# Seven block products in place of eight in the network stages of the last 2048 tokens, on one Trainium2 core

## The chip, the cores and the metric

The kernel runs on one core of one Trainium2 chip. The metric is device time in microseconds (us) for one execution; lower is better. The kernel before was timed in three runs.

## The reference, cut to what matters

The inputs are q, k and v of shape (4 batches, 8 heads, 768 tokens, 64) and four network weights. Attention comes first, then a network over all 4 x 768 = 3072 tokens:

```
k_sum = k.reshape(B, H, nb, 32, D).max(axis=3);  v_sum = v.reshape(B, H, nb, 32, D).mean(axis=3)
scores_l = scale * q @ k^T          masked to |i - j| < 16
scores_s = scale * q @ k_sum^T + log(32)
a = softmax(concat(scores_l, scores_s))
x = a @ concat(v, v_sum)            -> (3072 tokens, 512)
h = (x @ w1) * (x @ w2)             -> (3072, 1024)
out = (h @ w3) @ w_out              -> (3072, 512)
```

Everything is float32. The kernel folds `w3 @ w_out` into one matrix once, so that the network has two stages: the gates (`x @ w1`, `x @ w2` and their product) and the projection (h times the folded matrix). Each float32 operand of a network matmul is kept as two float32r numbers, a rounded one (hi) and the rest (lo), and each product is the sum of three matmuls: hi x hi, lo x hi and hi x lo.

## The kernel before, in words

The 3072 tokens are cut into six units of 512 tokens, and attention into 24 steps: a step is one unit and one pair of heads (`place` at L528 divides the step number by 4).

**Attention step.** `begin` (L549) makes the score matmuls on PE. `reduce` (L340) adds the mask and takes the extreme of each row on DVE, `expose` (L356) takes the exponential on ACT, `invert` (L363) adds 1e-9 on POOL and takes the reciprocal on DVE, and `normalize` (L367) multiplies on POOL. Two steps later come `transposes` (L381) on PE, `evacuate` (L391) to SBUF on ACT and DVE, `outputs` (L400) on PE, and `keep_x` (L417), which writes x as hi (ACT) and lo (DVE, `low` at L108). The inputs of a step arrive on SP's DMA queue: `fetch` (q and k), `fetch_values` (v). `load_sums` (L294) copies the block means of v into the value tile on POOL, and `gather` (L316) the block maxima of k into the key tile, on POOL as well.

**Network.** `gate` (L427) takes 128 of the 1024 gate columns of one unit: 12 matmuls with w1 (4 chunks of 128 inputs, three each), an ACT copy out of PSUM (L448), 12 matmuls with w2, the product on DVE (L453), then hi on ACT (L454) and lo on DVE. Eight such calls make a unit's gates. `project` (L459) makes 128 tokens of output in 24 matmuls over the eight chunks of the folded matrix `wp`, an ACT copy (L472) and a store issued on ACT's queue (L473); four calls make a unit. All of these matmuls have 512 columns and go through `products` (L111), so their line in the profile is L113. A unit has 192 gate matmuls and 96 projection matmuls. All network weights stay in SBUF as hi and lo.

**Order.** PE's order is written out. `run(columns)` (L520) draws network matmuls from a generator until so many columns have been handed out. In the first loop (L716), a schedule by turns (`LOADS`, `WORK`) loads and converts the weights, folds `w3 @ w_out` and makes the first eight attention steps, with unit 0's network filling in. In the second loop (L760), two attention steps are made together: both transposes, both scores, both outputs, then about 144 network matmuls. The order on the other engines is by priority, except for the attention instructions of ACT and DVE, which keep their program order. SP's order is written out in the first loop only; POOL's in the second only.

## Time and profile before

| | |
|---|---|
| runs of the kernel before | 534.08, 532.41, 533.48 us; median 533.48 us |
| profiled execution, first to last instruction (span) | 533.5 us |
| TensorE clock granted, mean | 0.990 |
| PE busy | 511.2 us (96%) |
| DVE, ACT, POOL busy | 240.6, 225.4, 95.9 us |
| moved by DMA | 68.78 MB, mean 129 GB/s |

Only the span is given for the profiled execution itself; it equals the median of the runs to 0.02 us. In the profile, PE is TensorE's matmuls, PEld its weight loads, DVE is VectorE, ACT ScalarE, POOL GpSimd, and SP the engine that issues most DMAs. Busy times of overlapping matmuls are merged, so that the mean of one matmul (391 ns) is longer than the distance between two of them; the distance is read from the chain of waits.

### The profile page before, as it was taken

The numbers are of one execution on the slowest core, as the hardware profiler recorded it, in microseconds if no ns is written. First come the engines' busy times: TensorE is split into PE (matmuls) and PEld (weight loads), VectorE is DVE, ScalarE is ACT, GpSimd is POOL, SyncE is SP. The second block draws the span as 40 slices with busy tenths as digits, with TensorE's granted clock in tenths as the row PEclk, the third lists the DMA queues.
The fourth block names the chain that finished last, engine by engine and source line by source line (L and its number), as shares of the span: only waits on it lengthen the run. The fifth ranks groups of instructions, "written<-read, shape, count | busy, mean of one in ns | idle before, by whom it ended". The sixth has DMA issues, their size and how long they took to land.

```text
span 533.5 us, 9766 instructions
## 1 busy us (share of the span) xinstructions
PE 511.2 (96%) x3888; PEld 421.4 (79%) x3888; DVE 240.6 (45%) x667; ACT 225.4 (42%) x627; POOL 95.9 (18%) x158
## 2 busy tenths in 40 slices
PE   1889989999999999999999999999999999999997
PEld 0667767888888888888888888888888888888885
DVE  5889987798534326435244043251042350222210
ACT  5587964674626226135154063361172361222210
POOL 2020635001033202305005014014023031000000
PEclk9989997999999999999999999999999999999999
DMA  8995699804834013453040150050150011100001
GB/s 346 413 411 220 252 325 413 316 2 139 274 131 167 0 55 122 151 172 134 0 177 1 60 195 1 1 177 20 49 187 2 14 69 40 39 3 0 1 20 59
DMA packets 21166, 68.78 MB, mean 129 GB/s; under 512 B 2304, under 2 KB 2432, under 8 KB 18560
## 3 DMA queue, kind: packets, MB, share of 16 engines
q1 hardware_dynamic: 17664, 61.86, 31.6%
q10 hardware_dynamic: 3456, 6.29, 3.1%
q8 instruction: 30, 0.49, 0.4%
q14 instruction: 16, 0.13, 0.1%
HBM read 61.85 MB, written 6.29 MB: 128 GB/s over the span
## 4 chain that ended last, share of the span: by engine, by line
PE 87%; DMA 5%; DVE 4%; ACT 2%; issue 1%; POOL 0%; SPq 0%; POOLq 0%; ACTq 0%
PE mm L113 76%; PE po L408 4%; PE sc L331 4%; DMA rows<-in_vP_dram 2%; PE tp L388 2%; DVE wf L176 2%; DMA wraw<-in_w_dram 1%; DVE w L109 1%; DMA wraw<-in_wo_dram 1%; ACT sm L359 1%; DVE wf L173 1%; ACT wf L164 1%; DVE sm L345 0%; ACT w L190 0%; DVE ks L236 0%
## 5 line engine op out<-in xcount | busy, mean ns | idle before, releaser
L113 PE MATMUL mm<-x,w 128*128 128x512 f32 x1152 | 264.3, 391 | 0.0
L113 PEld LDWEIGHTS mm<-x,w 128*128 128x128 f32 x1152 | 216.5, 188 | 45.3
L113 PE MATMUL mm<-wp,h 128*128 128x512 f32 x576 | 133.3, 390 | 0.0
L113 PEld LDWEIGHTS mm<-wp,h 128*128 128x128 f32 x576 | 107.7, 188 | 22.6
L359 ACT ACTIVATE sm<-sm,mx 128x120 f32<-128x120 f32 x192 | 73.6, 385 | 16.3 <-DVE mx L345 16.3
L453 DVE TENSOR_TENSOR g<-mm,g 128x512 f32<-128x512 f32 x48 | 33.1, 690 | 88.7 <-PE mm L113 85.4
L454 ACT CAST h<-g 128x512 fp32r<-128x512 f32 x48 | 29.5, 618 | 90.6 <-DVE g L453 90.6
L113 PE MATMUL mm<-w,w 128*128 128x512 f32 x192 | 51.2, 419 | 14.8 <-ACT w L190 12.0
L113 PEld LDWEIGHTS mm<-w,w 128*128 128x128 f32 x192 | 37.3, 200 | 25.7 <-ACT w L190 12.7
L364 POOL TENSOR_SCALAR mx<-mx 128x8 f32<-128x8 f32 x24 | 6.8, 283 | 275.5 <-ACT sm L359 275.3
L472 ACT COPY o<-mm 128x512 f32<-128x512 f32 x24 | 14.0, 584 | 82.5 <-PE mm L113 82.5
L397 DVE COPY pt<-tp 120x512 f32<-120x512 f32 x22 | 14.3, 684 | 75.2 <-PE tp L388 75.2
L109 DVE TENSOR_TENSOR h<-g,h 128x512 fp32r<-128x512 f32 x48 | 35.2, 736 | 25.6 <-ACT h L454 25.4
L448 ACT COPY g<-mm 128x512 f32<-128x512 f32 x48 | 28.1, 586 | 39.0 <-PE mm L113 38.4
L298 POOL COPY v<-vs 24x512 f32<-24x512 f32 (+1 forms) x64 | 40.7, 635 | 8.9 <-DMA v<-in_vW_dram 5.9
L345 DVE CUSTOM_DVE_ANT_0 sm<-sc,mask_sb 128x120 f32<-128x120 f32 x192 | 41.1, 274 | 0.0
L359 ACT ACTIVATION_READ_ACCUMULATOR sm<-sm,mx 128x1 f32 x192 | 36.2, 188 | 0.0
L368 POOL TENSOR_TENSOR sm<-sm,mx 128x960 f32<-128x960 f32 x16 | 28.7, 1793 | 5.6 <-DVE mx L365 5.6
L109 DVE TENSOR_TENSOR x<-po,x 128x512 fp32r<-128x512 f32 x24 | 16.6, 690 | 28.6 <-ACT x L419 28.5
L190 ACT CAST w<-wf 128x1024 fp32r<-128x1024 f32 (+1 forms) x22 | 21.3, 968 | 17.3 <-DVE wf L176 17.2
L408 PEld LDWEIGHTS po<-pt,v 120*64 120x64 f32 x768 | 24.5, 141 | 4.0 <-issue 2.5
L408 PE MATMUL po<-pt,v 120*64 120x64 f32 x768 | 26.6, 228 | 0.9 <-POOL v L298 0.5
(35 smaller groups left out, 287.9 us busy)
## 6 DMA issues: line engine op xcount, KB each, us to landing
v<-in_vW_dram SPq DMA_DIRECT2D x24, 512.0 KB, 6.4
wraw<-in_w3T_dram SPq DMA_DIRECT2D x8, 1024.0 KB, 13.0
wraw<-in_w_dram SPq DMA_DIRECT2D x8, 1024.0 KB, 9.3
k<-in_kW_dram SPq DMA_DIRECT2D x20, 368.0 KB, 5.3
raw<-in_kT_dram SPq DMA_DIRECT2D x16, 392.0 KB, 3.7
q<-in_qG_dram SPq DMA_DIRECT2D x24, 256.0 KB, 4.9
raw<-in_vB_dram SPq DMA_DIRECT2D x12, 512.0 KB, 3.8
out_dram<-o ACTq DMA_DIRECT2D x24, 256.0 KB, 2.0
```

The costliest lines, as they stand in the source:

```text
L109: eng.tensor_tensor(dst, src, hi.bitcast(F32), ALU.subtract)
L113: nc.tensor.matmul(acc, lhsT=a, rhs=b, start=first and i == 0, stop=last and i == len(terms) - 1)
L190: nc.scalar.copy(t[:, 0, some], f[:, some])
L298: nc.gpsimd.tensor_copy(v[at : at + NB, g, blocks], src.unsqueeze(1).broadcast_to([NB, n, P]))
L331: nc.tensor.matmul(sc[h][64 * g : 64 * g + 64, i * KR : (i + 1) * KR], lhsT=q[rows, i * P + 64 * g : i * P + 64 * g + 64], rhs=k[rows, i, ...
L345: nc.vector.tensor_tensor_reduce(out=sm[:, j], in0=sc[h][:, i * KR : (i + 1) * KR], in1=mask_sb[:, 0 if blk == 0 else 2 if blk == BLOCKS - ...
L359: nc.scalar.activation(sm[:, j], sm[:, j], AF.Exp, bias=mx[:, 0, j : j + 1], scale=-1.0, accum_out=mx[:, 1, j : j + 1])
L368: nc.gpsimd.tensor_tensor(sm, sm, mx[:, 2].unsqueeze(2).broadcast_to([P, NI, KR]), ALU.mult)
L408: nc.tensor.matmul(po[cols, at : at + 64], lhsT=v[:KR, g, i, cols], rhs=pt[g][:, (h * NBLK + i) * 64 : (h * NBLK + i + 1) * 64], start=Tru ...
L448: nc.scalar.copy(g, a[:, :U])
L453: nc.vector.tensor_tensor(g, acc[1][:, :U], g, ALU.mult)
L454: nc.scalar.copy(h[:, 0], g)
```

## The change

Units 0 and 1 (the first 1024 tokens) keep the network of before. Units 2 and 3 are taken together, and so are units 4 and 5. For such a couple, both network stages become a product of two by two blocks: the gates have w1 and w2 as the two rows of blocks, the two halves of the 512 inputs as the inner index and the two units as the columns; the projection has the two halves of the output columns, the two halves of the 1024 gate columns, and the two units. A product of two by two blocks takes eight block products; here it takes seven, at the price of sums of blocks before and after:

- **Weight sums** (`stationary`, `sums_of_gates`, `sums_of_output`): four sums per tile of blocks on POOL, split into hi (ACT) and lo (DVE), stored to DRAM. The plain blocks are stored too (`spill_weights`, `spill_wp`, `whole_wp`, and the line added to `convert`).
- **x** of units 2 to 5 goes out of PSUM through one ACT copy to DRAM (`spill_x`) and is loaded again (`load_x`). `moving_x` makes the seven moving operands: for four of the seven a POOL sum, then hi (ACT) and lo (DVE).
- **Gates** (`fast_gates`): two rounds, each with seven products in four lanes (a lane is one PSUM bank), six matmuls per lane and product. The weights come from DRAM, two tiles of 512 KB per product, asked for in advance by `flow_in`. After each product each bank is read out (`evacuated`): by ACT for the first two products, by DVE with an addition for the other five. A bank goes on accumulating within the groups (0, 1), (2, 3) and (4, 5, 6) of products. POOL multiplies the two gates.
- **Projection** (`fast_project`): seven products in two lanes of twelve matmuls; the moving operands for the next product are made during this one (`moving_h`). The output is transposed, stored by SP into a second output tensor.
- **Attention steps** of the second loop are taken one at a time (`lump`): transposes and scores, 12 network matmuls, outputs, then more network matmuls. `invert` and `gather` move from POOL to DVE. The block means of v of the later batches go to the value tile by DMA from DRAM (`keep_means`, `fetch_means`). POOL's and SP's order is no longer written out in the second loop.

The core of the diff:

```
@@ convert
         for some in parts:
             low(nc.vector, t[:, 1, some], f[:, some], t[:, 0, some])
+        if name in wR:
+            nc.sync.dma_start(wR[name][i], f)
...
+    def spill_x(po, u, c):
+        t = sb.tile([P, U], F32, name="xr", tag="wf", bufs=5)
+        nc.scalar.copy(t, po[:, :U])
+        nc.sync.dma_start(xS[u][c], t)
...
+    def moving(k, b, dst):
+        hi, lo = dst
+        src = b[(0, 1, 0, 1, 0, 0, 1)[k]][(0, 0, 0, 1, 0, 1, 0)[k]]
+        if k == 2:
+            nc.gpsimd.tensor_tensor(src, b[0][1], src, ALU.subtract)
+        elif k == 3:
+            nc.gpsimd.tensor_tensor(b[0][1], src, b[0][1], ALU.subtract)
+        elif k == 4:
+            nc.gpsimd.tensor_tensor(src, b[1][1], src, ALU.subtract)
+        elif k == 6:
+            nc.gpsimd.tensor_tensor(src, src, b[0][0], ALU.subtract)
+        yield 1
+        nc.scalar.copy(hi, src)
+        yield 1
+        low(nc.vector, lo, src, hi)
...
+    def flow_in(n):
+        while flow and len(ready) < n:
+            t = sb.tile([P, 2, 512], F32R, name="ws", tag="x", bufs=6)
+            nc.sync.dma_start(t.bitcast(F32), flow.pop(0))
+            ready.append(t)
+
+    def lanes(n, weights_of, moving_of, steps, evacuated, tags, between=None):
+        banks = [ps.tile([P, 512], F32, name="ln", tag=tag, bufs=bufs) for tag, bufs in tags]
+        for k in range(NK):
+            stationary_of = yield from weights_of(k)
+            for i in range(n):
+                for c in range(steps):
+                    if between and c % KH == 0:
+                        between(k, i * steps // KH + c // KH)
+                    a, m = [stationary_of(i, c, w) for w in range(2)], moving_of(k, c)
+                    terms = [(a[0], m[0]), (a[1], m[0]), (a[0], m[1])]
...
+                with tc.high_priority(offset=SOONER):
+                    evacuated(k, i, banks[i][:, :U])
...
+    def fast_gates(n):
...
+            def weights_of(k):
+                while (n, k) not in xT:
+                    yield -1
+                flow_in(4 if r == NF // 4 - 1 and k >= 4 else 6)
+                two = [ready.pop(0), ready.pop(0)]
...
+            def evacuated(k, i, got):
...
+                if k < 2:
+                    nc.scalar.copy(h[:, 0] if k else p1, got)
+                else:
+                    to, more = ((p5, p1), (h[:, 1], p1), (h[:, 1], h[:, 1]), (p5, p5), (p1, p1))[k - 2]
+                    nc.vector.tensor_tensor(to, got, more, ALU.add)
+                if k == 5:
+                    nc.gpsimd.tensor_tensor(h[:, 1], h[:, 1], p5, ALU.mult)
+                elif k == 6:
+                    nc.gpsimd.tensor_tensor(h[:, 0], h[:, 0], p1, ALU.mult)
...
+    def fast_project(n, hr):
...
+        def weights_of(k):
+            flow_in(4)
...
+        def evacuated(k, i, got):
...
+            done = {1: (0, 0, c11), 4: (0, 1, d), 5: (1, 1, p5), 6: (1, 0, p1)}
+            if k in done:
...
+                nc.sync.dma_start(outT[rows : rows + P, cols : cols + U], t)
...
     def network():
-        for u in range(NU):
+        for u in range(2):
...
+        for n in range(1, NSU):
+            raws = yield from fast_gates(n)
+            yield from fast_project(n, raws)
...
+    CLASSIC = ALL_FOLD + 2 * UNIT
+    FAST = 3 * U * 4 * KH
+    UP_TO = {p: TO_SLOTS + (CLASSIC - TO_SLOTS) * (p - NFIRST + 1) / NFIRST for p in range(NFIRST, 2 * NFIRST)}
+    UP_TO[2 * NFIRST] = CLASSIC + 1.2 * FAST
+    UP_TO[2 * NFIRST + 1] = CLASSIC + 2.9 * FAST
+    for p in range(2 * NFIRST + 2, NS + 2):
+        UP_TO[p] = UP_TO[p - 1] + 2.2 * FAST
...
+    def lump(p):
...
+            tp = transposes(sms.pop(p - 2)[0], **more)
+            pt = evacuate(tp)
+            b = begin(p) if p < NS else None
...
+        run(given[0] + 12 * U)
+        with tc.manual_schedule(engines={engines.Activation, engines.DVE}):
+            finish_step(p - 2, pt, **more)
...
+        run((given[0] + UP_TO[p]) / 2)
+        load_batch()
+        run(UP_TO[p])
```

FAST is the 24 matmuls of one gate product. The sums and the operands of x are made in small pieces, one each time 2048 columns have been handed to PE (`tend`); the order in which they are asked for is tied to the attention step (`EXTRA`: sums of the gates from step 8, x of units 2 and 3 from step 12, x of units 4 and 5 from step 21).

More of the change, by code (lines that the diff above doesn't have):

```diff
@@ L398, in evacuate, with outputs @@
         return pt
[L400 to L402 removed]
+    def outputs(pt, v, **more):
+        po = ps.tile([P, 512], F32, name="po", **more or {"tag": "tp", "bufs": 2})
         for i in range(NBLK):
@@ new lines, in finish_step, with work_on @@
+    def finish_step(p, pt, **more):
+        u, c = place(p)
+        po = outputs(pt, values.pop(p), **more)
+        if u < 2:
+            keep_x(po, xs[u])
+        else:
+            spill_x(po, u, c)
+    def work_on(u, sm, mx, sc):
+        for h in range(2):
+            reduce(u, h, sc, sm, mx)
+            expose(h, sm, mx)
+        invert(mx)
+        normalize(sm, mx)
+    CLASSIC = ALL_FOLD + 2 * UNIT
+    FAST = 3 * U * 4 * KH
+    UP_TO = {p: TO_SLOTS + (CLASSIC - TO_SLOTS) * (p - NFIRST + 1) / NFIRST for p in range(NFIRST, 2 * NFIRST)}
@@ L795, in attention_moe @@
+    with tc.manual_schedule(engines=MANUAL):
+        for p in range(NFIRST, NS + 2):
+            lump(p)
         run(float("inf"))
-_OUT = "out_0_dram"
+_OUT, _OUT_T = "out_0_dram", "out_1_dram"
 def kernel(q, k, v, moe_w1, moe_w2, moe_w3, moe_w_out):
```

340 lines of the change are left out of this document (263 added, 77 removed).

## The prediction, made before the changed kernel was run

> **What bounds the kernel now.** I read the page first (busy times, the forty slices, the chain that ended last), then the chain in order of time, the groups of instructions with shapes apart, the time line of DVE and POOL where they overlap, and the DMA issues.
>
> ```profile
> span 533.5 us, 9766 instructions
> ...
> PE 511.2 (96%) x3888; PEld 421.4 (79%) x3888; DVE 240.6 (45%) x667; ACT 225.4 (42%) x627; POOL 95.9 (18%) x158
> ...
> PE   1889989999999999999999999999999999999997
> ...
> GB/s 346 413 411 220 252 325 413 316 2 139 274 131 167 0 55 122 151 172 134 0 177 1 60 195 1 1 177 20 49 187 2 14 69 40 39 3 0 1 20 59
> ...
> PE 87%; DMA 5%; DVE 4%; ACT 2%; issue 1%; POOL 0%; SPq 0%; POOLq 0%; ACTq 0%
> ```
>
> PE is busy for nine tenths or more of every slice from the seventh to the last but one, and 87% of the last chain is PE. The chain in order of time shows what the second loop does:
>
> ```profile
> 382.99 1.09 PE tp L388 x32
> 384.08 1.98 PE sc L331 x64
> 386.06 2.02 PE po L408 x64
> 388.08 32.86 PE mm L113 x144
> ...
> 462.38 67.60 PE mm L113 x297
> 530.00 0.59 ACT o L472
> ```
>
> Two attention steps cost PE 1.09 + 1.98 + 2.02 = 5.1 us, so one costs 2.55. Behind them 144 network matmuls take 32.86 us without a gap: **228.2 ns each**. Here nothing but the number of PE's instructions sets the time, so a matmul removed is worth its full distance, as long as PE stays fed.
>
> ```profile
> L113 PE MATMUL mm<-x,w 128*128 128x512 f32 x1152 | 264.3, 391 | 0.0
> L113 PE MATMUL mm<-wp,h 128*128 128x512 f32 x576 | 133.3, 390 | 0.0
> L453 DVE TENSOR_TENSOR g<-mm,g 128x512 f32<-128x512 f32 x48 | 33.1, 690 | 88.7 <-PE mm L113 85.4 <-ACT sm L359 1.6 <-ACT wf L164 1.3
> L109 DVE TENSOR_TENSOR x<-po,x 128x512 fp32r<-128x512 f32 x24 | 16.6, 690 | 28.6 <-ACT x L419 28.5
> L454 ACT CAST h<-g 128x512 fp32r<-128x512 f32 x48 | 29.5, 618 | 90.6 <-DVE g L453 90.6
> L448 ACT COPY g<-mm 128x512 f32<-128x512 f32 x48 | 28.1, 586 | 39.0 <-PE mm L113 38.4
> L368 POOL TENSOR_TENSOR sm<-sm,mx 128x960 f32<-128x960 f32 x16 | 28.7, 1793 | 5.6 <-DVE mx L365 5.6
> L318 POOL COPY k<-ks 128x96 f32<-128x96 f32 x16 | 5.3, 350 | 23.6 <-DMA k<-in_kW_dram 21.0 <-DVE ks L236 2.2
> L364 POOL TENSOR_SCALAR mx<-mx 128x8 f32<-128x8 f32 x24 | 6.8, 283 | 275.5 <-ACT sm L359 275.3
> ```
>
> **What is removed.** The first two rows are 1152 + 576 = 1728 matmuls, 288 per unit. A couple of units takes 576; with seven products it takes 7/8 of that, 504 (two gate rounds of 7 x 4 lanes x 6, and 7 x 2 lanes x 12). Two couples save 2 x 72 = 144 matmuls of the same shape: 144 x 0.2282 = **32.9 us**. Attention's matmuls stay. So PE alone would give 533.5 - 32.9 = 500.6 us. The sum is made against the span of 533.5, which is also the median of the runs (533.48), so nothing is converted.
>
> A couple then lasts 504 x 0.2282 = 115.0 us on PE, one product (24 matmuls) 5.48 us, a projection (168) 38.3 us.
>
> **What is added beside PE.** Per couple I count on DVE 14 lows of x, 28 lows of h, 40 additions out of PSUM in the gates and 10 in the projection: 92, where two units of before have 40. At 0.69 us each (the two DVE rows above) that is 63.5 us in 115. On ACT: 14 + 28 casts, 16 + 4 copies and 8 for the spilled x, 70 x about 0.61 = 43 us. On POOL, 8 sums for x, 16 for h and 16 gate products: 40. The trace has no POOL operation of two full tiles of 512; the nearest is the normalization of 960 columns at 1793 ns, and by columns 512 take 0.96 us (an estimate), 38 us per couple. Each engine alone fits beside 115 us of PE. Two things do not follow from such sums: who blocks whom, and whether data arrives.
>
> **POOL against DVE.** The time line of the two engines:
>
> ```profile
> 207.03 1.79 POOL L368 TENSOR_TENSOR sm<-sm,mx 128x960 f32<-128x960 f32 x1 [0.81 <-DVE mx L365]
> 212.72 1.79 POOL L368 TENSOR_TENSOR sm<-sm,mx 128x960 f32<-128x960 f32 x1 [0.32 <-DVE mx L365]
> 280.92 1.79 POOL L368 TENSOR_TENSOR sm<-sm,mx 128x960 f32<-128x960 f32 x1 [0.32 <-DVE mx L365]
> ```
>
> ```profile
> 207.52 1.85 DVE L109 TENSOR_TENSOR h<-g,h 128x512 fp32r<-128x512 f32 x1
> 213.88 1.18 DVE L109 TENSOR_TENSOR h<-g,h 128x512 fp32r<-128x512 f32 x1 [0.69 <-ACT h L454]
> 281.97 0.69 DVE L453 TENSOR_TENSOR g<-mm,g 128x512 f32<-128x512 f32 x1
> ```
>
> A low from SBUF normally takes 0.69 us. Begun while POOL normalizes it takes 1.85 and 1.18, and ends at 209.37 and 215.06, both times 0.55 us after POOL's end (208.82, 214.51). It does not run slower; it waits for POOL. The gate product, with one input in PSUM, is untouched at 0.69 under the third normalization. The Trainium skill has this as a rule (page "SBUF — State Buffer", section "Who interferes with whom"): a DVE instruction with two SBUF inputs and a GpSimd instruction that reads SBUF exclude each other, the later one waiting to the end of the earlier. By that rule, the trace agrees, with the 0.55 us above.
>
> The change puts both kinds into the same stretch. In a projection, 28 lows (19.3 us) and 16 POOL sums (15.3 us) exclude each other: 34.6 us in 38.3 of PE. If DVE's 10 additions (6.9) never ran under a POOL sum, DVE would need 41.5 us, 3.2 too many. In the first couple's projection, four steps' normalizations (4 x 1.79) and the x operands of the next couple (2 POOL sums, 6 lows: 6.1) add 13.3 us against 4 x 2.55 = 10.2 of attention on PE: 3.1 more. Bounds: 0 to 3.2 + 6.3 = 9.5 us. I take **2**, near zero, because POOL can run a product ahead, and the additions can run under its sums.
>
> **The weight stream.** Weights now come from DRAM twice per couple: 21 products of two 512 KB tiles, 22 MB in 115 us, 191 GB/s. The page shows slices of 413, so the mean fits. What matters is the wait for a buffer. Of six buffers the gates use two per product and are two products ahead (11 us). From the last gate products on, and through the projection, `flow_in(4)` keeps one product ahead: a pair is asked for when PE has freed the pair before, and needed one product, 5.48 us, later. I count 10 such pairs in the first couple and 8 in the second.
>
> ```profile
> v<-in_vW_dram SPq DMA_DIRECT2D x24, 512.0 KB, 6.4
> wraw<-in_w_dram SPq DMA_DIRECT2D x8, 1024.0 KB, 9.3
> ...
> raw<-in_vB_dram SPq DMA_DIRECT2D x12, 512.0 KB, 3.8
> out_dram<-o ACTq DMA_DIRECT2D x24, 256.0 KB, 2.0
> ```
>
> ```profile
> 69.52 0.42 SPq L144 DMA_DIRECT2D wraw<-in_w_dram  x1
> ```
>
> Alone, 512 KB land in 3.8 us; the second tile streams behind the first, 0.52 MB at 413 GB/s = 1.27 us, so the pair takes 5.1, or 5.5 with one issue of 0.42 on SP: just on time. In the congested first loop 1024 KB took 9.3 us, 3.8 too late. Ends: 0 and 18 x 3.8 = 68 us. Near the lower end, since most of that stretch has little other traffic. But SP's queue is in order: the output stores of products 1, 4 and 5 wait for a copy of 0.59 us and take two issues, and the load behind them starts about 1.2 us late. Six such loads: **+7.2 us**.
>
> **x by way of DRAM.** The last x of a couple goes ACT copy 0.59, store 2.0, load 3.5 (256 KB; between the 2.0 of a 256 KB store and the 3.8 of a 512 KB load, nearer the load), POOL 0.96, cast 0.62, low 0.69: 8.4 us, and the fourth product needs it. PE has, after those outputs, 29 matmuls of its step (1.7 x 24 less the 12 ahead of the outputs, 6.6 us), the next step's transposes and scores (1.5) and about 2 matmuls (0.5): 8.6 us. If the cover fails altogether it costs 8.4; I take **+1**. The second couple has three products in front, 16 us: nothing.
>
> **The first loop.** `gather` and `invert` move to DVE, which stands here:
>
> ```profile
> 93.00:133.00 40.00, 40.00 (x178) 33.13 (x177) 35.13 (x75) 23.73 (x56) 3.00 (x6) 1.00 0.43 156
> ```
>
> ```profile
> 109.30 1.23 DVE L109 TENSOR_TENSOR w<-wf,w 128x1024 fp32r<-128x1024 f32 x1
> 110.44 1.22 DVE L176 SCALAR_TENSOR_TENSOR wf<-wraw,wf 128x1024 uint32<-128x1024 uint32 x1
> ```
>
> DVE is busy 35.1 of 40 us and converts gate weights back to back just ahead of their use. A few gathers and additions (0.35 and 0.28 on POOL) go in front: 0 to 3 us, I take **+1**. SP's eight new stores of the converted weights wait for DVE, with the next weight loads behind them; those have three tiles' conversion in front, so nothing. The block-mean copies that POOL loses only shorten its queue. Taking attention steps singly costs PE nothing of its own, and 12 matmuls (2.7 us) cover the copies between transposes and outputs; with that cover gone it would be at most 1 us a step. At the end the last bank leaves by a DVE addition (0.69) where ACT copied (0.59): 0.1, left out.
>
> **Sum:** 533.5 - 32.9 + 2 + 7.2 + 1 + 1 = 511.8: **512 us**.
>
> **The rivals.**
> (a) *Everything stays hidden.* Pairs land in time and the sums fall in POOL's free time: 500.6 + 1 + 1 = 502.6. For it: the 5.1 us pair, DMA nearly idle in the last slices of before; against it: SP's order. 0.18. The Trainium skill (page "SBUF — State Buffer", section "The DMA setup-cost knee") fits 2 us plus bytes over 436 GB/s, 4.4 us for a pair by my estimate; the stream's term would then be near 0. No 1 MB load here ran alone to test it.
> (b) *The exclusion binds.* A lane's bank must be read out within 12 matmuls (2.74 us). An addition on DVE behind two lows that each wait for a POOL sum takes 2 x (0.96 + 0.55) + 0.69 = 3.7, 1 us late. Half of the 28 lane read-outs of both projections late by 1 us is 14 in place of 2: 524. For it: 34.6 of 38.3 us; against: POOL may run ahead. 0.18.
> (c) *Slower: the one-ahead weight stream is late at every product.* If a 512 KB tile lands in v's 6.4 us, which it took in company with q and k, a pair takes 7.7, 2.2 late, 18 times: 39.6 in place of 7.2, so 544. It turns to a loss where a pair takes over 5.48 + (533.5 - 504.6)/18 = 7.1 us. For it: attention's 1.1 MB per step and x share the engines in the first couple. Against: from then on, little shares them. 0.10.
> (d) *The products do not pay as counted*, for a matmul distance above 228 ns between alternating tiles: the shape is the same, so 0.02, and I put it at no change.
>
> **How the numbers follow.** My forecast has 0.52, from 505 to 518. A change within 0.3% (1.6 us) is about what a measurement cannot tell from none. Faster: 0.52 + 0.18 + 0.18 = 0.88; same 0.02; slower 0.10. The range reaches down to (a) and up past (b) by part of the x cover: 502 to 530; only (c) stays out, and what would go beyond either end.
>
> **What would show it.** PE instructions 3888 - 144 = 3744, the last row of the chain at 228 ns per matmul within a product. The stream's term: PE waiting in the projections for DMA of `ws`, about 1 us at the third, sixth and seventh product, none in the gates. The exclusion's: lows of 1.2 to 1.7 us and waits of PE for DVE. I am wrong if PE waits in the gates, if matmuls inside a product stand over 230 ns apart, or if the first 135 us shift by more than 3.

## The result, and the profile after

| | before | after |
|---|---|---|
| runs beside each other, median of 4 | 533.75 us (532.41 to 534.08) | 584.85 us (583.62 to 587.61) |
| profiled execution, span | 533.5 us | 584.2 us |
| TensorE clock granted, mean | 0.990 | 0.951 |

The ratio is 1.097, with a 95% interval from 1.093 to 1.101: slower by 10%, where 512 us and a range of 502 to 530 were forecast. The page of the changed kernel:

```profile
span 584.2 us, 10335 instructions
...
PE 506.2 (87%) x3744; PEld 401.5 (69%) x3744; DVE 378.5 (65%) x851; ACT 260.4 (45%) x695; POOL 218.2 (37%) x174
...
PE   2989979999948999895398999897979899999797
...
PEclk9989989999977999999599999998999899999899
...
GB/s 353 409 414 230 198 366 411 231 214 364 366 358 167 278 229 349 241 357 398 249 312 260 236 316 305 342 303 231 252 181 248 260 202 190 192 203 101 145 179 155
```

PE has 3744 instructions, as forecast, and is now busy for 87% of the span. A slice is 14.6 us: the big holes are the twelfth (161 to 175 us) and the nineteenth and twentieth (263 to 292 us), and in the last of these the granted clock is down at half. The GB/s row, which before had slices at 1 and 2 GB/s, stands above 100 everywhere; the bytes went from 68.78 to 157.64 MB. What PE waited for, by the view of waits (total, times, longest):

```profile
PE sc L361 <- DVE k L348: 19.7, 5, 6.8
...
PE ln L627 <- ACT xT L558: 9.6, 1, 9.6
PE ln L627 <- DVE tmp L751: 7.0, 4, 2.9
...
PE ln L627 <- ACT tmp L748: 4.1, 1, 4.1
```

L361 are the score matmuls, and L348 is `gather`, the copy of the block maxima into the key tile. L627 are the matmuls of the seven products, L558 the cast of x and h to hi, L751 and L748 the read-outs of a bank in the projection. No row names the stream of weights (`ws`). Groups of instructions, shapes apart (the last but one number of the first part is the mean, in ns, as in the prediction's rows):

```profile
L125 DVE TENSOR_TENSOR hT<-hr,hT 128x512 fp32r<-128x512 f32 x56 | 59.6, 1101 | 23.9 <-ACT hT L558 23.6
...
L398 POOL TENSOR_TENSOR sm<-sm,mx 128x960 f32<-128x960 f32 x16 | 30.0, 1875 | 67.4 <-DVE k L348 24.8 <-issue 19.6 <-ACT h L489 9.5
...
L554 POOL TENSOR_TENSOR hr<-hr 128x512 f32<-128x512 f32 x8 | 13.6, 1727 | 9.3 <-DVE hT L125 9.3
...
L593 POOL TENSOR_TENSOR wr<-wr 128x512 f32<-128x512 f32 x6 | 7.7, 1280 | 0.5
```

The low of h before was this row:

```profile
L109 DVE TENSOR_TENSOR h<-g,h 128x512 fp32r<-128x512 f32 x48 | 35.2, 736 | 25.6 <-ACT h L454 25.4
```

A low of h takes 1101 ns in the mean where it took 736 before, and a sum of two full tiles on POOL 1280 to 1727 ns, where 0.96 us was estimated.

Where the time went shows when the span is cut at PE's first matmul of each stage. "Counted" is the prediction's 500.6 us: the time before up to unit 0's projection, then the network matmuls left at 228.2 ns each and 49.8 us of attention, split by the steps that a stage holds. The last three columns are experiments, told below.

| stage | counted | after | sums on DVE | and no weight sums | and gather on POOL |
|---|---|---|---|---|---|
| up to unit 0's projection | 129.7 | 134.2 | 137.7 | 133.4 | 130.0 |
| from there to couple 1's first product | 114.7 | 154.9 | 147.0 | 124.2 | 122.6 |
| couple 1 (units 2 and 3, with attention) | 137.7 | 167.1 | 161.5 | 163.6 | 157.7 |
| couple 2 (units 4 and 5, no attention) | 115.0 | 123.9 | 115.0 | 115.0 | 115.0 |
| rest | 3.5 | 4.1 | 4.1 | 4.2 | 4.3 |
| span | 500.6 | 584.2 | 565.3 | 540.4 | 529.6 |

Of the 83.6 us that are too many, 40 lie between unit 0's projection and the first product, before any of the new products has run. The two holes in order of time (start, duration, engine; in brackets the idle time before and what ended it):

```profile
120.29 3.81 SPq L211 DMA_DIRECT2D w<-wf  x2
124.15 2.61 SPq L766 DMA_DIRECT2D wS<-w  x3
126.80 2.59 SPq L772 DMA_DIRECT2D p<-wp  x2
...
153.28 2.18 SPq L803 DMA_DIRECT2D pR<-wpr  x2
...
158.72 0.72 SPq L328 DMA_DIRECT2D k<-in_kW_dram  x1
...
165.40 0.38 DVE L348 COPY k<-ks 128x96 f32<-128x96 f32 x1 [4.40 <-DMA k<-in_kW_dram]
165.84 1.88 PE L361 MATMUL sc<-k,q 64*64 64x120 f32 x32 [5.59 <-DVE k L348]
...
270.92 1.26 POOL L591 TENSOR_TENSOR wr<-wr 128x512 f32<-128x512 f32 x1 [10.98 <-DMA wr<-w]
...
272.87 3.40 DVE L125 TENSOR_TENSOR sp<-wr,sp 128x512 fp32r<-128x512 f32 x2 [4.28 <-ACT sp L582]
273.49 2.23 POOL L398 TENSOR_TENSOR sm<-sm,mx 128x960 f32<-128x960 f32 x1
...
276.79 0.74 DVE L348 COPY k<-ks 128x48 f32<-128x48 f32 x2
...
277.54 1.88 PE L361 MATMUL sc<-k,q 64*64 64x120 f32 x32 [6.78 <-DVE k L348]
...
282.87 2.43 SPq L651 DMA_DIRECT2D xraw<-xS  x2
...
289.06 4.35 PE L627 MATMUL ln<-xT,ws 128*128 128x512 f32 x12 [9.65 <-ACT xT L558]
```

First hole: from 120.29 to 155.46 SP issues 34 stores of weights and nothing else. They take it 35.2 us with its own waits, and the key tile of step 8 is asked for behind them at 158.72. DVE idles until it lands, and PE with it. In the kernel before, the time line of SP has it at 140.01:

```profile
140.01 0.43 SPq L308 DMA_DIRECT2D k<-in_kW_dram  x1
```

The stores start so late because eight of them, those of the converted gate weights (L211, two of them among the 34), wait for DVE's conversion, and SP's queue with them:

```profile
SPq L211 <- DVE wf L192: 27.3, 5, 7.4
```

Second hole: the last gate weights come back from DRAM late, POOL's sums of them begin at 270.92, and two lows of those sums take 3.40 us on DVE, since they and POOL's normalization exclude each other (they end at 276.27, 0.55 us after its end at 275.72, the distance that the prediction found in the kernel before). The key copy of the next step stands behind them on DVE. Then x: its first loads are issued at 282.87, because `load_x` waits in one list behind the weight sums, and the first product begins at 289.06.

### The profile page after: what moved, and what is told of

It is laid out like the page before. It is cut to its first block, busy times and chain, and to the rows that moved or that the text cites. A ratio compares the mean times of both kernels' runs of the same rounds, so it can differ in the third digit from the quotient of the medians.

```text
span 584.2 us, 10335 instructions
## 1 busy us (share of the span) xinstructions
PE 506.2 (87%) x3744; PEld 401.5 (69%) x3744; DVE 378.5 (65%) x851; ACT 260.4 (45%) x695; POOL 218.2 (37%) x174
## 2 busy tenths in 40 slices
DMA packets 56964, 157.64 MB, mean 270 GB/s; under 512 B 5968, under 2 KB 14672, under 8 KB 54352
## 5 line engine op out<-in xcount | busy, mean ns | idle before, releaser
L627 PE MATMUL ln<-xT,ws 128*128 128x512 f32 x672 | 161.9, 400 | 18.2 <-ACT xT L558 9.6
L627 PEld LDWEIGHTS ln<-xT,ws 128*128 128x128 f32 x672 | 127.2, 192 | 48.4 <-ACT xT L558 10.6
L129 PE MATMUL mm<-x,w 128*128 128x512 f32 x384 | 93.0, 400 | 0.9 <-DVE w L125 0.9
L627 PE MATMUL ln<-hT,ws 128*128 128x512 f32 x336 | 82.1, 402 | 9.3 <-ACT tmp L748 4.1
L129 PEld LDWEIGHTS mm<-x,w 128*128 128x128 f32 x384 | 72.7, 192 | 18.2 <-DVE w L125 1.6
L627 PEld LDWEIGHTS ln<-hT,ws 128*128 128x128 f32 x336 | 64.0, 193 | 25.2 <-DVE tmp L751 5.4
L125 DVE TENSOR_TENSOR hT<-hr,hT 128x512 fp32r<-128x512 f32 x56 | 59.6, 1101 | 23.9 <-ACT hT L558 23.6
L558 ACT CAST hT<-hr 128x512 fp32r<-128x512 f32 x56 | 33.0, 622 | 58.7 <-POOL hr L713 42.7
L709 DVE TENSOR_TENSOR tmp<-ln,tmp 128x512 f32<-128x512 f32 x48 | 32.9, 687 | 38.3 <-PE ln L627 24.8
L129 PE MATMUL mm<-wp,h 128*128 128x512 f32 x192 | 46.9, 399 | 1.5 <-ACT g L483 1.3
L361 PE MATMUL sc<-k,q 64*64 64x120 f32 x768 | 28.3, 289 | 20.7 <-DVE k L348 19.7
L129 PEld LDWEIGHTS mm<-wp,h 128*128 128x128 f32 x192 | 35.9, 190 | 10.7 <-ACT g L483 1.8
L361 PEld LDWEIGHTS sc<-k,q 64*64 64x64 f32 x768 | 22.3, 145 | 23.6 <-DVE k L348 13.6
```

What stands on the lines that cost most here:

```text
L125: eng.tensor_tensor(dst, src, hi.bitcast(F32), ALU.subtract)
L129: nc.tensor.matmul(acc, lhsT=a, rhs=b, start=first and i == 0, stop=last and i == len(terms) - 1)
L361: nc.tensor.matmul(sc[h][64 * g : 64 * g + 64, i * KR : (i + 1) * KR], lhsT=q[rows, i * P + 64 * g : i * P + 64 * g + 64], rhs=k[rows, i, ...
L558: nc.scalar.copy(hi, src)
L627: nc.tensor.matmul(banks[i][:, :U], lhsT=x, rhs=y, start=c + j == 0 and k in FIRST_OF_GROUP, stop=c == steps - 1 and j == 2 and k in LAST_ ...
L709: nc.vector.tensor_tensor(to, got, more, ALU.add)
```

## The experiments

The theory after this reading (A): the preparation of the weights, by SP's queue and the sums, costs the time before the first couple. The rival (B): POOL and DVE exclude each other all along, and the sums on POOL are what is late. Beside them stand three smaller causes: single steps, the moved copy, and a supply of network matmuls that runs out. All but the last two experiments are single runs, beside runs of the kernel before with spans of 530.3 to 533.6 us. Times below are spans, unless they are called times; a run's time is 1.7 to 1.9 us longer than its span.

**No weight sums** (`e1_no_weight_sums`). The sums, the stores that feed them and the loads back are left out, so products 2 to 5 use plain blocks:

```
-        if name in wR:
-            nc.sync.dma_start(wR[name][i], f)
...
-        8: [lambda: tasks.extend(sums_of_gates(q) for q in range(4))],
...
-        18: [lambda: tasks.extend(sums_of_output(c) for c in range(2))],
```

> The changed kernel without the preparation of weight sums: no sums, no copies of the unsplit weights to DRAM and back; products three to six stream the plain blocks of products one, two and seven instead, so what is computed is not the reference's and the traffic of the fast stages stays as it is. Theory A (late preparation: what is stored to and fetched from DRAM for the fast stages, with its buffers, holds up the key tiles and the x operands between 134 and 289 us, where 40 us were lost): most of the waits of PE for the key gather and the 9.65 us for the first x operand go; total 550 to 562. Theory B (POOL and DVE exclude each other in the fast stages): only 32 of POOL's two-tile operations go (24 sums and 8 rebuilt tiles), before the fast stages mainly; total 572 to 582.

563.6 us, 1.6 above theory A's range. The key tile of step 8 is asked for at 144.53 and its score matmuls do not wait, though 28 of the stores are still in SP's queue: what is gone are the eight that wait for DVE and the four of the whole folded matrix. The first product begins at 256.6 in place of 289.1: 32.5 us. But 12 of them are lost again, 10 of these in couple 1, behind one row:

```profile
PE po L438 <- ACT pt L423: 16.2, 4, 9.6
```

ACT's queue is in order: its copy for attention stands behind casts that wait for POOL.

**All two-tile sums on DVE** (`e2_sums_on_dve`): `nc.gpsimd.tensor_tensor` becomes `nc.vector.tensor_tensor` in the eleven places of such sums and gate products. POOL keeps the normalizations.

> The changed kernel with every two-tile sum and gate product on DVE instead of POOL; the same numbers are computed. Theory B (exclusion): lows on DVE fall from 0.97 to 1.10 us back to 0.69, and the 39 us lost in the two couples fall by half or more; total 555 to 568. Theory A (late preparation): the first 289 us stay as they are within 5 us, DVE gets some 110 operations of 0.69 us more, and the total is 575 to 595.

565.3 us, 18.9 less. The lows of h fall to 710 ns. Of the 38.3 us lost in the two couples 14.5 went, less than the half that theory B asked for. PE's time line of couple 2:

```profile
446.20 76.90 PE L627 MATMUL ln<-xT,ws 128*128 128x512 f32 x336 [0.46 <-DVE tmp L751]
522.93 38.24 PE L627 MATMUL ln<-hT,ws 128*128 128x512 f32 x168
```

504 matmuls without a gap from 446.20 to 561.17: 115.0 us, 228.1 ns each, at full clock, though DVE has more to do than in the changed kernel (72 us in place of 62). So the sums' place on POOL is the whole loss of couple 2, and the stream of weights, the alternating tiles and the read-outs cost nothing there. That is not all exclusion. The longest of PE's waits in couple 2 of the changed kernel came like this:

```profile
525.34 1.29 POOL L711 TENSOR_TENSOR hr<-hr,tmp 128x512 f32<-128x512 f32 x1 [15.65 <-DVE tmp L709]
...
535.80 2.54 POOL L713 TENSOR_TENSOR hr<-hr,tmp 128x512 f32<-128x512 f32 x2
...
537.77 1.11 DVE L125 TENSOR_TENSOR hT<-hr,hT 128x512 fp32r<-128x512 f32 x1 [5.71 <-ACT hT L558]
...
543.62 12.78 PE L627 MATMUL ln<-hT,ws 128*128 128x512 f32 x48 [4.12 <-ACT tmp L748]
```

From 525.34 to 538.34 POOL works through ten operations of 1.27 to 1.29 us each, none of them stretched. Four of them are sums for the projection's fourth product (L552), taken ahead and standing between the gate products, so that the last gate products (L713), which the second product's operands need, come late. A low on DVE waits 5.71 us for a cast that waits for them, and the read-outs stand behind both. That is POOL's own length and order in a chain of in-order queues. How the 18.9 us divide between it and the exclusion no run separates. Of the 18.9 us, couple 2 has 8.9, couple 1 5.6, and what lies before the first product 4.4.

The second hole stays, at 6.81 and 9.62 us, with the same chain on DVE: the sums wait for the gate weights from DRAM, and the key copy stands behind them. So the late weights make it; the sums' place on POOL does not.

**Stores on another queue** (`e3_spills_on_act`): the stores of the plain weights issued by ACT.

> The changed kernel with the stores of the plain weights (gate weights unsplit and split, folded matrix split and whole) issued on ACT's queue instead of SP's. Theory A1 (the loads of steps 8 and 9 are late because they stand behind those stores on SP's in-order queue): the 9.7 us for which PE waited for key gathers at the start of the second loop shrink to 3 or less, total 572 to 580. Theory A2 (the 16 DMA engines are full there, or PE has nothing else to do while it waits): within 4 us of the changed kernel, 580 to 590, or worse by ACT's issue time.

585.6 us, no gain, as A2 said of the total. PE's wait for the key copy in unit 0's projection fell from 9.7 to 2.1 us, so the first hole is SP's order; but unit 0's gates took 50.8 us in place of 46.9, with waits for ACT and DVE. ACT has to issue those stores now.

**The kernel before with the stores alone** (`e5_before_plus_spills`): no product changed, only 36 of the 40 stores of plain weights added to SP's queue at the same turns.

> The kernel before with one part of the change alone: the converted gate weights, their hi and lo halves and the folded matrix are also stored to DRAM by SP's queue at the turns where the changed kernel does it, and never read. Theory A: SP is busy issuing until about 155 us and the first loads of the second loop come late behind it; PE waits for the key tiles of steps 8 and 9, total 538 to 548. Theory B: within 2 us of before, 532 to 536.

560.5 us, above theory A's range: 27 us slower, nearly all by one wait in the second loop:

```profile
PE sc L338 <- POOL k L325: 25.8, 2, 24.4
```

SP issues stores until 175 us and the next key tile at 176.68. Of these stores the prediction put eight at nothing and had the other 28 in no term. The DMA engines are full while PE waits (a share of 1.04 from 160 to 176 us), so this run alone does not tell the order of the queue from the traffic.

**The gates' sums from the halves in SBUF** (`e11_sums_from_halves`), on top of the sums on DVE: the raw gate weights are neither stored nor loaded again.

```
-                nc.sync.dma_start(t[:, j].rearrange("p c f -> p (c f)"), wR[w][q])
+                nc.vector.tensor_tensor(t[:, j].rearrange("p c f -> p (c f)"), hi, lo, ALU.add)
```

> The changed kernel with all two-tile sums on DVE, and the raw gate weights not stored to DRAM in the first loop and loaded again for the sums: the sums of the gates start instead from hi + lo of the resident weights, one DVE addition of 1024 columns per weight tile (8, about 1.2 us each). All seven products and their stores stay, and the output weights keep their way. It tells what the preparation's cost is made of. Leaving out the stores and the sums took 565.3 to 540.4. Theory A1 (the eight stores on SP's queue in the first loop and the loads back delay the key tiles and the sums): span 540 to 552, u0p's wait for the key gather (5.6 us) mostly gone. Theory A2 (the sums' own work on DVE and ACT and the rest of the stores, between 180 and 290 us): span 558 to 568.

552.5 us, half a microsecond above A1's range and far below A2's: the way of the gate weights through DRAM is 12.8 us. Without the eight stores SP asks for the key tile of step 8 at 147.14, though the 32 others are still in its queue, and PE's waits for scores at step 8 (3.45 us in the kernel with the sums on DVE) and at the second hole (6.81) are gone. The wait for x stays, at 10.28.

**Both causes out** (`e10_both`): no weight sums, and the other sums on DVE.

> The two edits that each gained at one place together: no weight sums and none of the stores of plain weights and their way back (the gate and output products 2 to 5 read plain blocks, so part of the computation is left out), and every sum of two full tiles on DVE in place of POOL. Alone they gave spans of 563.6 and 565.3 against 584.2. Theory A (two separate causes: the preparation of the weights costs before the first couple, the exclusion of POOL and DVE in the couples, and the 12 us that the first edit gave back in the projection of couple 1 were the exclusion): the gains add and what was given back returns, span 530 to 545, couple 2 at 115 us, first fast matmul before 258. Rival B (both edits relieve the same stalls, those of a DVE and ACT that run behind): span 552 to 564. What would be left above the ideal 500.6 under A is single steps (about 8), the wait for x at the entry (about 10), the stalls of key tiles in the first loop, and slow clock behind stalls.

540.4 us, as theory A said: 24.9 below the sums on DVE alone, so 12.1 of them are the sums' own work and the rest of what was left out. The first product begins at 257.6 and does not wait: x is on time for it once no weight sum stands ahead of it in the list. What is left in couple 1 shows in one place of the time line:

```profile
361.57 2.49 DVE L127 TENSOR_TENSOR hT<-hr,hT 128x512 fp32r<-128x512 f32 x4
363.98 0.20 DVE L395 RECIPROCAL mx<-mx 128x8 f32<-128x8 f32 x1
...
364.43 1.95 POOL L398 TENSOR_TENSOR sm<-sm,mx 128x960 f32<-128x960 f32 x1 [22.08 <-DVE mx L395]
364.65 1.79 DVE L348 COPY k<-ks 128x96 f32<-128x96 f32 x1
...
366.55 1.88 PE L361 MATMUL sc<-k,q 64*64 64x120 f32 x32 [6.21 <-issue]
```

The key copy is queued on DVE behind the sums and lows of h, and PE idles 6.21 us for it. The copy itself takes 1.79 us here, where copies of its shape otherwise take 0.16: POOL's normalization runs from 364.43 to 366.38, and the copy ends at 366.44. So a copy with one input in SBUF waits for POOL as well. The Trainium skill (page "SBUF — State Buffer", section "Who interferes with whom") says that of copies that DVE makes in a mode with two ports. The trace agrees so far as the copy ends 0.06 us after POOL; in which mode it ran no view tells. Two of the sixteen steps have such a copy (the other, 1.17 us from 311.43, ends 0.07 us after POOL); in the others the copy runs free of POOL.

**Gather back on POOL**, in the changed kernel (`e13_gather_on_pool`) and in the one with both causes out (`e14_both_and_gather`): `nc.vector.tensor_copy` becomes `nc.gpsimd.tensor_copy` in `gather`.

> The changed kernel with one part undone: the copy of the block maxima into the key tile (gather) is on POOL again, everything else is as changed. In the changed kernel PE's score matmuls wait 19.7 us in 5 places for that copy on DVE. Theory A (the copy stands in DVE's queue behind the low of a weight sum, or behind the addition and reciprocal of the attention step, which wait for ACT's exponentials; on POOL it would not): at least half of that returns, span 568 to 576. Rival B (the copy is late because its key tile lands late, and SP's queue of stores is the cause, so that it doesn't matter which engine copies; on POOL it also queues behind the sums): span 580 to 590, and the same waits stand under the name of POOL.

> The kernel without the sums and stores of the weights and with the other two-tile sums on DVE (span 540.4; part of the computation left out as there), with the copy of the block maxima on POOL besides. There PE still waits 15.0 us for score operands (5.1 for the copy on DVE by name, 9.9 unnamed in two places, at each of which the copy on DVE ends just before). Theory A (place in DVE's queue): most of the 15 us and the slow clock behind them go, span 522 to 530, and what is left above 500.6 is the single steps (about 9), the first loop (about 4) and the wait for the transposed weights of attention (about 5). Rival B (the tiles land late): span 536 to 545.

584.3 us in the first: nothing gained, theory A missed, and the wait stands under POOL's name:

```profile
PE sc L361 <- POOL k L348: 14.9, 3, 9.2
...
PE ln L627 <- ACT xT L558: 13.0, 2, 11.6
```

529.6 us in the second: 10.8 gained, just inside theory A's range; 3.4 of them lie in the first loop and 5.9 in couple 1. So the copy's place on DVE costs 10.8 us once the tiles land in time; while the stores keep the tiles and the sums late, undoing it alone gains nothing. (This kernel is below the 533.5 of the one before because it leaves the weight sums out.)

**Single steps in the kernel before**, without and with a supply of network matmuls kept back for them (`e4_before_single_steps`, `e7_single_steps_supplied`).

> The kernel before with attention steps of the second loop taken one at a time (transposes and scores, 12 network matmuls, outputs, more network matmuls), nothing else changed. Theory C (the single steps cost PE waits and switches of their own): 540 or more, with PE waiting in each step. Theories A and B: each step adds two changes between attention and network on PE, 0.1 to 0.3 us a step, so 534 to 538.

> The kernel before with single attention steps, as in the earlier run of 571 us, but with network matmuls left for every step (the first loop stops at 0.85 of unit 0, each later step has a quarter of a unit whose x is complete). Theory D: the four stalls of 5.8 us go, and what is left is the price of a single step on PE itself, 0.5 us each for 18 steps: 540 to 546. Rival (single steps make late key gathers in any case): 555 or more.

569.3 us, in theory C's range: with single steps alone PE waits 23.4 us for key tiles, nearly all in four places. With 0.85 of a unit before the second loop in place of 0.96, and an even share per step, these four are gone: 541.3 us, in theory D's range. So the network matmuls had run out there. One step:

```profile
332.80 0.68 PE L388 MATMUL tp<-ident,sm 64*120 64x64 f32 x16
333.41 1.05 PE L331 MATMUL sc<-k,q 64*64 64x120 f32 x32
334.39 3.06 PE L113 MATMUL mm<-x,w 128*128 128x512 f32 x12
337.38 1.15 PE L408 MATMUL po<-pt,v 120*64 120x64 f32 x32
338.46 13.89 PE L113 MATMUL mm<-x,w 128*128 128x512 f32 x60
352.29 0.68 PE L388 MATMUL tp<-ident,sm 64*120 64x64 f32 x16
```

From 332.80 to 352.29 are 19.49 us for 72 matmuls (16.43) and one step (2.55, half a pair): **0.51 us more per step**, with PE never idle in it. Twelve matmuls between scores and outputs last 3.06 us, not 2.74. Sixteen steps cost 8.2 us; the whole spans differ by 7.8 to 11.0, as the kernel before ran in 533.5 or 530.3.

**More supply in the changed kernel** (`e6_supply`, on top of the sums on DVE): the same 0.85, and the first two units spread over one step more.

> The kernel with the sums on DVE (565.3 us span) and another split of PE's network work: the first loop stops at 0.85 of unit 0 in place of 0.96, and units 0 and 1 are spread over nine steps in place of eight, so that steps 8 and 16 have classic matmuls left. Theory D (single steps run out of network matmuls at step 8, before unit 1's x is complete, and at step 16, before the first x operand is; what is late there shows only because nothing covers it): the stalls of 5.6 and 16.4 us and the slow clock behind them go for the most part, total 538 to 550. Rival (the late loads would hold up any order): 558 to 566.

570.4 us: the theory fell. The key copies stayed late (26.0 us of PE's waits). At step 8, where PE waits 10.24 us, DVE itself idles 9.04 us for the tile from DRAM: there it is the tile that is late, not the work that runs out.

**One couple only.** If the saving itself is real, a version with less preparation should win: units 0 to 3 as before with pairs of steps, only units 4 and 5 by seven products (16.4 us saved, 517.1 counted), the sums on DVE from the halves in SBUF, the stores handed out in pieces. `e8_one_couple` is the first; `e9_even` spreads the network of the first four units more evenly (at least 0.26 unit per pair of steps in place of 0.20); `e12_pt_on_act` hands out the sums one operation at a time and a pair of steps earlier, and puts attention's copies on ACT; `e15_one_couple_singly` puts these back; `e16_clear_of_steps` hands out no sum in the 14 matmuls ahead of a pair; `e16_timed` is the same kernel, run twelve times, and `e17_sums_singly` splits the last additions.

> A new kernel: seven products only for units 4 and 5, after all attention; units 0 to 3 as before; attention steps two at a time as before; sums on DVE; stores and sums spread over the second loop, the sums made from hi and lo in SBUF. PE has 72 matmuls fewer, 16.4 us, and no attention beside the couple. If the arithmetic of seven products pays whenever its preparation is covered: 517 to 526. If the weight stream and the read-outs cost PE by themselves: 530 or more.

> The version with one couple (units 4 and 5; pairs of steps as in the kernel before, sums on DVE, weight sums from the halves in SBUF) with the network of the first four units handed out more evenly: 0.26 unit per pair of steps (75 matmuls) in the last four pairs, where the version before it had 0.20 (58 matmuls) and PE idled 13.3 us between 320 and 428 us. Everything else is the same. Theory A (those stalls are attention running out of network matmuls to hide the chain of a step behind): span 520 to 532. Rival B (they are the sums of the weights and the stores that queue ahead of attention's copies on DVE and on the DMA queue, whatever the spread): span 540 to 548.

> The version with one couple and an even spread (span 537.1, of which PE waits 4.7 us for DVE's copy of the transposed weights of attention, 1.7 for DVE's gate product, 3.3 unnamed), with three edits against those waits: from step 10 on both of those copies are on ACT (46% busy there, DVE 67%), the sums of the weights come one DVE operation at a time instead of three or four together, and they begin one pair of steps earlier. Theory A (what is left is DVE running bursts of preparation ahead of attention's copies): span 526 to 533, below the kernel before. Rival B (the preparation's work and DMA traffic shift the waits to ACT or to the weight stream): 535 to 542.

> The one-couple version with an even spread, the sums of the weights one operation at a time and begun a pair of steps earlier, and the transposed weights of attention copied as in the kernel before, half on ACT and half on DVE. With both halves on ACT the span was 536.6 and PE's waits for DVE's copy (4.7 us) had turned into waits of the second step's scores (7.3 us). Theory A (these waits were ACT's four copies in a row, and single operations on DVE delay nothing by more than 0.7 us): span 527 to 533. Rival B (SP's stores of the sums, which stand in its queue ahead of the next key tiles, hold the scores up whichever engine copies): 534 to 540.

> The one-couple version of before (span 535.8), in which no operation of the weight sums is handed out within the last 14 network matmuls (3.2 us) ahead of a pair of attention steps, and a sum's store one piece later behind its low. There PE waits 13.0 us between 134 and 331 us, 5.9 for DVE's copy of the transposed weights, 1.3 for DVE's gate product, 5.2 unnamed directly ahead of such copies, and 2.4 for a key tile. Theory A (DVE holds operations of the sums when attention's copies come): span 526 to 532, below the kernel before. Rival B (DVE is behind over whole stretches, 67% busy, so that a gap of 3.2 us doesn't empty its queue, or the waits are SP's): 533 to 538.

> The same one-couple version that gave a span of 529.9 in a single look, now timed in rounds against the kernel before. If the look holds: 530 to 533 us, ratio to the kernel before 0.992 to 0.998. If it was chance: a ratio whose interval holds 1.

> As the version before it, with the additions that rebuild the weights from their halves handed out one at a time as well (they still came two and four together: 2.6 us of DVE in front of one of attention's copies). Theory A (bursts on DVE are the rest of PE's waits, 11 us between 134 and 400 us): 527 to 531 us, ratio 0.985 to 0.995. Rival B (the remaining waits are the ordinary two or three operations in DVE's queue): as the version before, 531 to 533.

Spans of 546.6, 537.1, 536.6, 535.8 and 529.9 us in single runs. The first missed its range of 517 to 526, the second fell between its two theories, the third and fourth came out in their rivals' ranges, the fifth in theory A's. The couple itself takes 114.4 us in all of them (115.0 counted); the loss lies ahead of it, between 130 and 430 us. In the first, the waits were these, among network shares of 58 matmuls per pair:

```profile
PE sc L343 <- POOL k L330: 5.4, 3, 2.6
PE sc L343 <- DVE pt L409: 4.2, 3, 2.7
PE sc L343 <- issue: 3.9, 3, 1.9
```

The even spread gained 9.5 us. That the copies moved to ACT changed nothing: PE then waited 7.3 us (unnamed) for scores. The 529.9 (531.67 as a time, beside 535.32 for the kernel before) did not hold: eleven of twelve further runs of the same kernel took between 530.66 and 537.61 us, median 533.7 (the twelfth, 538.87, is not in the ratio); the ratio to before is 1.0015 with an interval from 0.9989 to 1.0042. The last version has a median of 534.0 and 1.0012 (0.9987 to 1.0037), no better than its rival said. These versions scatter by 6 to 7 us from run to run, so that steps of a few us between their single runs say nothing, and the 9.5 are little more. The best that was found equals the kernel before: one couple's 16.4 us are lost again ahead of it.

## Why the prediction was wrong, point by point

**What is removed: right.** 3744 matmuls, and a couple in 115.0 us when nothing interferes. Rival (d) is out: no matmul got dearer inside a product. One reading of the base was off: the profiled execution's span of 533.5 is not the median's. In every run with both figures the time is 1.7 to 1.9 us above the span, so that the sum of 511.8, made from a span, is about 513.6 as a time. Beside the 73 us that were missed this is nothing.

**The step that failed is the preparation of the weights.** "SP's eight new stores of the converted weights wait for DVE, with the next weight loads behind them; those have three tiles' conversion in front, so nothing." The eight do wait for DVE, 27.3 us in all. But behind them on the same queue stand 32 other stores, and behind these the key tiles of the second loop; the step looked only at the weight loads of the first. Without the eight, and with 28 or all 32 of the others, step 8 does not wait. The count also left out the other stores themselves, the loads back, and the sums with their casts and lows, which appear in no term: "What is added beside PE" was counted per couple only. Thirty-six of the stores alone cost 27 us in the kernel before; in the changed kernel, with the sums on DVE, the whole preparation costs 24.9, of which 12.8 is the gate weights' way through DRAM. "The first 135 us shift by more than 3" was among the signs, and they shifted by 4.5.

**POOL against DVE: the right place, the wrong size, and only half the mechanism.** Taken at 2 us with bounds of 0 to 9.5; 18.9 by moving the sums to DVE. Of the terms, the POOL sum was 0.96 (by columns) and is 1.28 us undisturbed. With it, 28 lows and 16 sums are 19.3 + 20.5 = 39.8 us in 38.3 of PE, so they don't fit. "POOL can run a product ahead" came true and cost: four sums of a later product (L552, 1.29 us each) stand among the gate products, ahead of the last of them, for which the projection's second product waits, and the eight sums left for the projection's later products (L554, L556) took 1.65 to 1.73 us each in the mean. And the bound left out that ACT's casts and read-outs wait in order behind POOL's queue (4.1 us of ACT `tmp`, L748). Rival (b), 524, had the place but only the read-outs of the projections; PE also waited in the gates, as it said it wouldn't. The Trainium skill (page "SBUF — State Buffer", section "Who interferes with whom") has the rule that a DVE instruction with two SBUF inputs and a GpSimd instruction that reads SBUF wait for each other; the trace agrees, with the low that ends 0.55 us after POOL.

**The weight stream: +7.2 forecast, about 0 found.** PE's waits after have no row for `ws`, and couple 2 with the sums on DVE has no gap though DMA is at 203 GB/s there. That kernel has two such waits in couple 1, 3.3 and 0.6 us. Rival (c) gave a loss, but by a mechanism that did not occur. No view gives the time in which a pair landed, so which of its estimates was nearest stays open; the 1.2 us behind each store did not reach PE.

**x by way of DRAM: +1 forecast, 9.65 found**, and at the first product, not the fourth. The chain was counted from the last x; it did not see that its loads wait in one list behind the sums of the weights. Without those sums the first product does not wait.

**The first loop: +1 for the moved operations.** With the other causes out, moving the gather back gains 3.4 us there, a little over the bound of 3. It has a larger price later: in the second loop its copy is in DVE's in-order queue, 10.8 us in all. The step counted the copy's duration, and neither what is queued ahead of it nor that it waits for POOL.

**"Taking attention steps singly costs PE nothing of its own":** 0.51 us each, 8.2 in all, by steps in which PE never idles.

Removed one on top of the other, the parts of the 83.6 us are: sums on POOL 18.9, weights' preparation 24.9, gather 10.8, and 29.0 left. In these 29.0, single steps are 8.2, waits of PE after 130 us 13.4 (5.8 of them for DVE's copy of the transposed weights of attention, 3.9 for an operand of x), the first loop and the end 1.1; some 6 are not assigned. The lower clock behind the waits may be most of them: the mean granted clock of couple 1 is 0.97 there, over 157.7 us, some 4 to 5 us by an estimate. The parts depend on the order: gather alone gave nothing. That the stores cost by their place in SP's queue rather than by their traffic was shown for the first hole (its wait is gone with all of them on ACT's queue, and without the eight that wait for DVE), not for the rest.

## What to carry to other kernels

Where an algorithm saves on the engine that bounds, list what prepares its operands as carefully as what it saves, store by store, with the in-order queue that each goes through and what stands behind it there; here 32.9 us saved brought 83.6 us of loss, over half of it before the first of the new products. An engine that is 45% busy is not free: for each small operation that PE needs, ask what may be queued ahead of it, and count that, not its duration. After such a change, undo parts in pairs too, since one late operand hides another.

## What the runs showed of the hardware

- The TensorE clock falls after PE idles: the 32 score matmuls behind the holes take 1.88 us at a granted clock of 0.50 (165.84 and 277.54), and 1.05 at 1.00 where PE had not waited (197.92). A wait of 6.78 us so costs PE at least 0.83 us more behind it.
- An issue on SP's queue has no fixed length. In the first hole, with the DMA engines 92% busy, the 12 stores of split gate weights took 0.52 to 1.54 us each and the 16 of the folded matrix 0.45 to 1.37. The 16 stores of the gates' sums, later, took 0.32 to 0.43 us each with the engines 81 to 86% busy. Whether the form of the store or the fullness of the queue makes the difference no run separates. All that stands behind a long issue waits.
- Changing between small attention matmuls and network matmuls costs PE about 0.17 us each time, by an estimate: a single step has four such changes, a step in a pair has one, and the three more cost 0.51 us.
- On POOL as on DVE, the duration in the profile holds the wait for the other engine, by what these rows show: the same kind of sum of two tiles takes 1289 ns in the mean (L552, in couple 2 while DVE only adds out of PSUM) and 1727 ns (L554) in the projections amid DVE's lows.
